# New settings for the virtual clock that orders a fused S4D convolution and channel MLP on one core

## The chip, the core and the metric

The kernel runs on one core of a Trainium2 chip. The metric is the time of one execution on the device in microseconds (us). The core has five engines with a queue each: TensorE (PE in the rows, with its weight loads as PEld), VectorE (DVE), ScalarE (ACT), GpSimd (POOL) and SyncE (SP), which here only starts transfers. An engine works its queue off in order; an instruction that has to wait for another engine or for a transfer holds up all that is queued behind it.

## The reference

For 2048 tokens of 576 channels, `u` is normalized; the normalized rows go through two branches whose product is added to the input:

```python
xn = layernorm(u)                                   # 2048 x 576
A, C = -exp(log_A_real) + 1j*A_imag, (C_real + 1j*C_imag) * dt[:, None]
K = 2 * einsum("dn,dnl->dl", C, exp(A*dt*pos)).real # a filter of 2048 taps for each channel
s = irfft(rfft(xn, 4096) * rfft(K, 4096))[:2048] + xn * D_skip
y = layernorm(xn)
h = gelu(y @ w1 + b1)                               # 576 -> 4608
g = silu(h @ w2 + b2)                               # 4608 -> 576
return u + s * g
```

Everything is float32.

## The kernel before

**The MLP.** The 4608 hidden channels are cut into 12 groups of 384 (`NG`, three blocks of 128 each, `G`), the tokens into two halves of 1024 and each half into two blocks of 512. A *slot* is one group on one block of 512 tokens: there are 48 (`NSLOT`). A slot has eleven *positions*. At the first three, `layer1` (line 633) multiplies a block of `w1` with the tokens, 14 matmuls of 512 columns each. At the other eight, `layer2` (line 707) multiplies the hidden block with `w2`, 72 matmuls of 288 columns in all. Float32 precision is made of two float32r parts, high and low: `w1h`/`w1l`, `XH`/`XL`, `w2h`/`w2l`, `hh`/`hl`. Between the layers ACT makes the GELU (671) and the high part (674), then DVE the low part `hl` (677). DVE adds every finished output to `acc` (717). The weights of each group come in raw and are split by ACT (586) and DVE (583).

**Pairs.** The last 64 of the 576 input channels hold their high part `XR[:64]` and low part `XR[64:]` in one tile. Line 633 therefore ends with two matmuls on `XR`, with `w1r` and with `w1s`. Where `pair` (616) has run before a slot, the first and the third block of this slot leave the `w1s` matmul out: two matmuls of 64 rows each, one on `XR`, one on a copy of its lower half in the tile `bias2`, have done this product already. A pair is made only at the edge of a slot, and only ahead of a visit to the convolution there.

**The convolution.** Between positions TensorE makes *visits*: `kgen` (1042) makes the filter for 16 channels from tables of cosines and magnitudes; `x1` (1157), `k1` (1188), `s2` (1217), `inverse` (1260) and `i1` (1286) transform 96 channels forth and back. Six chunks of 96 channels give 74 visits. A `kgen` may *ride* along in the visit of another kind. The tables are made by DVE (lines 963 to 1003) and ACT (969 to 982); their parameters come by `load_par` (944), started by POOL. The results of a visit go out of PSUM by ACT and by DVE transposes (1165, 1196) or products (1234, 1240). In front of all this stand the layernorms: `BN_STATS` and `BN_AGGR` (423, 425) on DVE, the scaling (466) on POOL.

**What sets the order.** All instructions are written out by the class `Order` before anything runs, and the order is pinned. It keeps a virtual clock for each engine and a price for each step (`dve`, `act`, `pool`, `LEN`); *lines* are chains of steps in order of rank. After each position `advance` lets every step run, in the order in which the clock says it becomes ready, that doesn't delay a more urgent one. `pe_turns` decides whether a visit goes in after a position: its operands must be ready by the clock with a margin, visits of `c1` are paced by `END`, a `kgen` that stands alone waits `ALONE` for company and by `DUE`. `HOLD` puts single steps back by hand. So each of these numbers can move instructions on all engines, and the instructions themselves stay as they are.

Of the kernel before, what the change touches and what calls it, by code (L numbers as in the profile page):

```python
# [32 lines left out]
G = 3  # L33
# [18 lines left out]
class Order:  # L52
# [44 lines left out]
    def take(self, eng, dur, ready, tbl=None):  # L97
        start = max(self.t[eng], ready)
        if eng == "DVE" and self.shared and start < self.t["POOL"] - 0.4:
            dur *= 1.1  # L100
        if tbl and tbl != self.tbl:
            dur += 1.28
            self.tbl = tbl
        self.t[eng] = start + dur
        return start + dur + self.LAT
# [119 lines left out]
def mixer_kernel(ctx, tc, u, log_a_real, a_imag, c_real, c_imag, log_dt, d_skip, w1, b1, w2, b2,  # L225
# [8 lines left out]
    def bank2(name):  # L234
        return ps.tile([P, 2, TB], F32, name=name, bufs=2 if name == "cv" else 1)
# [373 lines left out]
    def pair(tb):  # L609

        Q1[0] = bank2(mx(1))
        for e, x in enumerate((XR[:64, tb], XQ[0][64:])):
            r, k = slice(64 * e, 64 * e + 64), e * (G - 1)
            nc.tensor.matmul(Q1[0][:, e], W[1][3][r, k * P:(k + 1) * P], x, start=True, stop=False,  # L616
                             skip_group_check=True)
        BEGUN.update((0, G - 1))
# [334 lines left out]
    def tables(b):  # L953
# [37 lines left out]
        def weigh(part):  # L991
# [10 lines left out]
            else:  # L1002
# [7 lines left out]
                 step("DVE", dve(SB * NV), f(phase, 0), need=[("kg", b - 2)] if b > 1 else []),  # L1010
                 step("DVE", dve(n), f(phase, 1), hold=HOLD.get(("phase", b), 0)), step("ACT", act(SB * NV), whole),
                 step("DVE", dve(SB * NV), frac, hold=HOLD.get(("frac", b), 0)), step("ACT", act(SB * NV), fold, mark=("fold", b))],
                [step("ACT", act(SB * NV), f(sin, 0), need=[("fold", b)], mark=("sin", b, 0), tbl="sin"),
# [3 lines left out]
                + [step("DVE", dve((2, 2, 1, 1)[part] * n), f(weigh, part), need=[("sin", b, 1)],  # L1017
                        mark=("wu", b) if part == 3 else None, hold=HOLD.get(("weigh", b, part), 0)) for part in range(4)])

# [49 lines left out]
        return behind  # L1069


    X1, S2, INV, I1, KG = 1.5, 1.75, 2.15, 3.05, 1.03

    HOLD = {("weigh", 19, 3): 1, ("phase", 19): 1, ("frac", 18): 2, ("k", 2, 1): (2, 1), (2, 0, 24): 1, (2, 1, 24): 1, ("k1", 2, 1, 2): 1}

    def chunk(c):

# [40 lines left out]
        def in_parts(which, i, get, m, need):  # L1118
# [19 lines left out]
            if which == "x":  # L1138
                four.append(step("ACT", act(2000), turn, need=need))
            hold = HOLD.get((which, c, i), (0, 0))  # L1140
            four.append(step("ACT", act(768), high, need=need if which == "k" else (), hold=hold[0]))
            four.append(step("DVE", dve(768), low, mark=(which + "p", c, i), hold=hold[1]))

        def x1(i):
# [18 lines left out]
            for d0 in (0, 24):  # L1163
                c0 = 48 * i + d0
                add("DVE", 0.9, lambda d0=d0, c0=c0: nc.vector.transpose(
                    A2[:, :, 0, c0:c0 + 24].rearrange("p k d r -> p d k r"), Q[d0]), cv=-1, hold=HOLD.get((c, i, d0), 0))

        def k1(i):
# [26 lines left out]
            for g in (0, 2):  # L1195
                add("DVE", 0.9, lambda g=g: nc.vector.transpose(
                    A2[:, :, 1, 48 * i + 12 * g:48 * i + 12 * g + 24].rearrange("p k d r -> p d k r"), Q[g]), cv=-1,
                    hold=HOLD.get(("k1", c, i, g), 0))

# [118 lines left out]
    NPOS = G + 8  # L1318
    NSLOT = 4 * NG
    od = Order(tc, nc)  # L1320
    od.pinned = True
    el, wl2, wl, nl2, pl, pl2, nl, ml, ml2, xl, wx, c3, c2, c1, c4, kl, tl, sl, vl, gl, odl, fl = [od.line() for _ in range(22)]
    nlh, mlh, mlt = od.line(), od.line(), od.line()
    od.lines = od.lines[-3:] + od.lines[:-3]

# [76 lines left out]


    L1 = 14 * 0.2315
    LEN = [L1] * G + [3 * n * 0.132 + 0.02 for n in (4, 2, 2, 4, 3, 3, 3, 3)]

    T0 = 12.5
    for e, t in dict(PE=0.0, ACT=4.6, DVE=3.7, POOL=3.8, SP=0.0).items():
# [71 lines left out]
    def weigh_in(which):  # L1480

        m = KB + 1 if which == 1 else G
        end = od.t["PE"] + sum(LEN[G:] if which == 1 else LEN[:G])
        for i in range(m):
# [90 lines left out]


    pace = dict(left=NCH * (2 + 2 + 4), last=0.0, started=False)
    END = 1000.0


    EDGE = 0.2, 0.6
    ALONE, DUE = 20.0, (160.0, 950.0)

    def pe_turns(limit=1, any_time=False, all_lines=True, edge=None):
        for x in (nl, pl, ml) + ((c3, c1, kl) if all_lines else ()):
            n = 0
            while n < (2 if x in (c1, nl) else limit):
                h = od.head(x)
                if h is None or h[0]["eng"] != "PE" or h[1] > od.t["PE"] + (0.3 if x is nl else -0.4):
                    break  # L1590
                if x is c1:
                    now = od.t["PE"]
                    gap = (END - now) / max(pace["left"], 1)
                    if n == 0 and pace["started"] and now < pace["last"] + EDGE[edge is None] * gap and not any_time:
                        break
                    pace["started"], pace["last"] = True, now
                    pace["left"] -= 1
                if x is kl and pace["started"]:
                    b = kl["steps"][0]["mark"][1]
                    wait = ("wu", b + 1) not in od.marks or od.t["PE"] < DUE[0] + b * (DUE[1] - DUE[0]) / NB  # L1600
                    if b < NB - 1 and od.t["PE"] < h[1] + (ALONE if wait else 3.0):
                        break
                if edge is not None and not BEGUN and x in (c3, c1, kl):
                    m = wmark(edge // 2, 1) + [("xq", edge)]
                    if all(k in od.marks and od.marks[k] < od.t["PE"] - 0.3 for k in m):
                        od.unit(lambda: pair(edge % 2), 0.24)
                behind = ride(h[0]) if x in (c1, c3) else None
                od.run(x)
                if behind:
                    behind()  # L1610
                od.pin()
                od.advance(od.t["PE"])
                n += 1

    LATER = {}

    def later(slot, pos, f):
        LATER.setdefault((slot, pos), []).append(f)
    mid = 2 * NG
# [19 lines left out]
    def when(pos, q):  # L1639

        return od.t["PE"] + sum(LEN[k % NPOS] for k in range(pos + 1, q))

# [28 lines left out]
    for slot in range(NSLOT):  # L1671
# [3 lines left out]
        n = slot // 2  # L1675
        final = slot >= NSLOT - 2
        for pos in range(NPOS):
            if pos < G:
# [9 lines left out]
                if pos == 2:  # L1688
                    BEGUN.clear()
                    k = slot % (2 * NG)  # L1690
# [16 lines left out]
            else:  # L1707
# [9 lines left out]
                halves = slot == NSLOT - 1 and j == 3  # L1717
                od.unit(lambda: cell.append(layer2(g, tb, j, terms, last, halves or 2 * (slot == NSLOT - 1 and j == 2))), LEN[pos] + 0.95 * (halves and not terms[0][1]), need)
                look_ahead(pos)
                b = 8 + 4 * tb + j  # L1720
                if halves:
                    dh = terms[0][1]
                    od.marks["z", dh] = od.t["PE"] + od.LAT
                    x = od.line()
# [3 lines left out]
                if split:  # L1728
                    add = cell[0]
                    for d in range(2) if j == 0 else (terms[0][1],):  # L1730
# [4 lines left out]
                        x = od.line()  # L1735
# [3 lines left out]
                if last and not halves:  # L1739
# [4 lines left out]
                    elif final:  # L1744
                        x = el if slot < NSLOT - 1 else od.line()
# [10 lines left out]
                if pos == NPOS - 1 and tb == 1 and slot + 1 < NSLOT:  # L1756
                    weigh_in(2)
            for f in LATER.get((slot, pos), ()):
                f()
            od.advance(od.t["PE"])  # L1760
            pe_turns(edge=slot + 1 if pos == NPOS - 1 else None, all_lines=pos in (0, 1, 2, G + 1, G + 3, G + 5, NPOS - 1))
    od.force(lambda: not od.urgent and not any(x["steps"] for x in od.lines))


# [52 lines left out]
```

## Time and profile before

| | |
|---|---|
| median of 3 runs | 1095.59 us (1095.1 to 1095.95) |
| the profiled execution, its own time | 1095.67 us |
| its span, first to last instruction | 1093.9 us |
| PE busy | 1087.1 us (99%) |
| DVE, ACT, POOL busy | 82%, 66%, 17% |
| granted TensorE clock | 0.999 |

The span lies inside the execution's own time, 1.77 us shorter. Matmuls overlap in the profile: the duration of one covers its whole way through the array, and the next starts earlier. What a matmul costs TensorE is the distance from its start to the next start. The timeline shows one instruction or a run of like ones a row, with its start, its duration and, in brackets, what ended an idle stretch before it.

### The profile page before, as it was taken

The page shows a single profiled execution, that of the slowest core. Times are in us where ns is not written, and L with a number is a line of the kernel's source. Part 1 is how long each engine was busy: PE and PEld are TensorE (multiplying, and loading weights), DVE is VectorE, ACT ScalarE, POOL GpSimd, SP SyncE. Part 2 cuts the span into 40 slices and gives each one's busy share as a digit, 9 for nine tenths or more (in the row PEclk, how much of TensorE's full clock was granted, in tenths as well). Part 3 has the DMA queues.
Part 4 walks back from the last instruction along what each step waited for, and adds up shares of the span by engine and source line. Part 5 has one row for each costly group of instructions (what it writes and reads, how often), then busy time and mean ns, then how long its engine had stood idle before and what let it go on. Part 6 is the DMA issues. An engine that isn't in the chain of part 4 may idle for free.

```text
span 1093.9 us, 27052 instructions
## 1 busy us (share of the span) xinstructions
PE 1087.1 (99%) x11445; PEld 954.0 (87%) x11445; DVE 891.9 (82%) x1302; ACT 727.1 (66%) x1113; POOL 188.4 (17%) x261
## 2 busy tenths in 40 slices
PE   9999999999999999999999999999999999999998
PEld 7989899899888898888988888888888888888897
DVE  7798667889998879889899987997969888766367
ACT  6585699778676674767767848685675757534333
POOL 4566210153020100001100000000001021101132
PEclk9999999999999999999999999999999999999999
DMA  8746764626354152355624215143142434454444
GB/s 242 225 149 152 236 235 143 179 80 157 116 160 134 44 112 67 96 110 148 161 48 118 78 56 141 34 122 87 56 126 42 144 101 132 114 170 150 137 151 103
DMA packets 139553, 138.22 MB, mean 126 GB/s; under 512 B 88952, under 2 KB 105016, under 8 KB 138856
## 3 DMA queue, kind: packets, MB, share of 16 engines
q1 hardware_dynamic: 124424, 85.05, 29.0%
q0 software_dynamic: 14528, 50.71, 14.7%
q8 instruction: 89, 1.46, 0.6%
q10 hardware_dynamic: 480, 0.74, 0.3%
q14 instruction: 32, 0.26, 0.1%
HBM read 102.17 MB, written 36.63 MB: 127 GB/s over the span
## 4 chain that ended last, share of the span: by engine, by line
PE 95%; DVE 3%; ACT 1%; SPq 1%; issue 0%; DMA 0%; POOL 0%; DVEq 0%; ACTq 0%; POOLq 0%
PE mxb L707 20%; PE mxa L707 20%; PE mxa L633 20%; PE mxb L633 20%; PE cv L1217 3%; PE cv L1042 3%; PE cv L1260 2%; PE cv L1286 2%; PE cv L1188 1%; PE cv L1157 1%; PE mxa L1348 1%; DVE acc L717 0%; PE mxa L648 0%; SPq L1089 0%; PE mxb L616 0%
## 5 line engine op out<-in xcount | busy, mean ns | idle before, releaser
L677 DVE TENSOR_TENSOR hl<-h,hh 128x512 fp32r<-128x512 f32 x144 | 98.5, 687 | 99.2 <-ACT hh L674 98.4
L707 PE MATMUL mxa<-w2h,hh 128*128 128x288 f32 x573 | 170.3, 297 | 0.0
L707 PE MATMUL mxb<-w2h,hh 128*128 128x288 f32 x573 | 170.2, 297 | 0.0
L707 PE MATMUL mxb<-w2h,hl 128*128 128x288 f32 x573 | 169.3, 295 | 0.1
L707 PE MATMUL mxa<-w2h,hl 128*128 128x288 f32 x573 | 169.1, 295 | 0.0
L707 PE MATMUL mxa<-w2l,hh 128*128 128x288 f32 x573 | 168.6, 294 | 0.0
L707 PE MATMUL mxb<-w2l,hh 128*128 128x288 f32 x573 | 168.6, 294 | 0.0
L671 ACT ACTIVATE h<-mxa,b1t 128x512 f32<-128x512 f32 x73 | 50.1, 687 | 98.3 <-PE mxa L633 95.1
L707 PEld LDWEIGHTS mxa<-w2h,hh 128*128 128x128 f32 x573 | 107.6, 188 | 5.8 <-issue 3.0
L707 PEld LDWEIGHTS mxb<-w2h,hh 128*128 128x128 f32 x573 | 107.6, 188 | 4.3 <-issue 1.4
L707 PEld LDWEIGHTS mxb<-w2l,hh 128*128 128x128 f32 x573 | 107.6, 188 | 0.8
L707 PEld LDWEIGHTS mxa<-w2l,hh 128*128 128x128 f32 x573 | 107.6, 188 | 0.6
L707 PEld LDWEIGHTS mxb<-w2h,hl 128*128 128x128 f32 x573 | 107.5, 188 | 0.3 <-DVE hl L677 0.3
L707 PEld LDWEIGHTS mxa<-w2h,hl 128*128 128x128 f32 x573 | 107.5, 188 | 0.0
L671 ACT ACTIVATE h<-mxb,b1t 128x512 f32<-128x512 f32 x71 | 48.8, 687 | 69.7 <-PE mxb L633 67.2
L674 ACT ACTIVATE hh<-h 128x512 fp32r<-128x512 f32 x144 | 90.7, 631 | 3.7
L944 POOL DMA_DIRECT2D par<-par_s x36 | 27.8, 771 | 367.8 <-DVE mg L988 325.0
L717 DVE TENSOR_TENSOR acc<-mxa,acc 128x576 f32<-128x576 f32 x87 | 65.5, 753 | 26.0 <-PE mxa L707 25.9
L717 DVE TENSOR_TENSOR acc<-mxb,acc 128x576 f32<-128x576 f32 (+1 forms) x89 | 65.9, 741 | 17.8 <-PE mxb L707 17.7
L633 PE MATMUL mxa<-XH,w1h 128*128 128x512 f32 x284 | 79.2, 401 | 0.0
L633 PE MATMUL mxb<-XH,w1h 128*128 128x512 f32 x280 | 77.7, 399 | 0.0
L633 PE MATMUL mxa<-XL,w1h 128*128 128x512 f32 x284 | 76.1, 390 | 0.0
(277 smaller groups left out, 2494.4 us busy)
## 6 DMA issues: line engine op xcount, KB each, us to landing
raw<-in_B_w_dram SPq DMA_DIRECT2D x72, 288.0 KB, 3.4
raw<-in_B_w_dram SPq DMA_DIRECT2D x96, 192.0 KB, 3.5
par_s<-A POOLq DMA_DIRECT2D x4, 2160.0 KB, 8.1
par<-par_s POOLq DMA_DIRECT2D x36, 240.0 KB, 3.6
f2t<-f2q SPq DMA_DIRECT2D x24, 256.0 KB, 3.6
g2t<-g2p SPq DMA_DIRECT2D x24, 256.0 KB, 4.1
bias<-XR SPq DMA_DIRECT2D x42, 128.0 KB, 3.6
raw<-in_B_w_dram SPq DMA_DIRECT2D x48, 96.0 KB, 3.7
```

Source lines behind the costliest of these rows:

```text
L633: nc.tensor.matmul(q, a, b, start=j == 0 and i not in BEGUN, stop=j == len(ops) - 1, skip_group_check=True)
L671: nc.scalar.activation(t, q, AF.Gelu_apprx_tanh, bias=b1t[:, k:k + 1], scale=1.0)
L674: LAST[0] = nc.scalar.activation(hh[:, i], t, AF.Copy)
L677: nc.vector.tensor_sub(hl[:, i], t, hh[:, i].bitcast(F32))
L707: nc.tensor.matmul(q[:, dh, :288], a[:, i, c], b[:, i, d], start=i == 0 and k == 0 and alone != 1, stop=i == G - 1 and k == 2, skip_group_ ...
L717: nc.vector.tensor_add(o, q[:, dh:dh + n, :288], b)
L944: nc.gpsimd.dma_start(PAR[b].rearrange("p (g i) k -> p g (i k)", g=4), dram(par_s, (b // 3 * 48 + b % 3 * 4) * NPAR, [[D * NPAR, P], [12 * ...
L1042: nc.tensor.matmul(q[32 * g:32 * g + 32, i // 2, i % 2 * 64:i % 2 * 64 + 64], U[:, ri, 4 * g + i, :], v[:, ri, 4 * g + i, :], start=ri == ...
L1157: nc.tensor.matmul(Q[24 * v][:, e], FP[0][r, f, 0], x[r, 12 * e:12 * e + 12], start=n == 0, stop=n == 2, skip_group_check=True)
L1217: nc.tensor.matmul(Q[i][32 * q:32 * q + 32, f, ri::2], m[r, 4 * i + q, 32 * ri:32 * ri + 32], A2[r, 4 * p + 2 * i + q // 2, :, :, q % 2], ...
L1260: nc.tensor.matmul(QI[q // 2][64 * f:64 * f + 64, q % 2, i], MAT["g2t", p + i // 2][r, i % 2, f, ri], YS[p + i // 2][0][r, i % 2, ri, f], ...
L1286: nc.tensor.matmul(Q[h][64 * y:64 * y + 64, t], g1t.rearrange("p a e -> p (a e)"), A2[:, k:k + 2, 1].rearrange("p i d r -> p i r d"), star ...
```

## The change

The numbers of the virtual clock are others. DVE beside POOL is priced at 1.05 instead of 1.1; three visit prices change (`X1` 1.55, `S2` 1.68, `INV` 2.34), and that of a pair (0.29); the seven entries of `HOLD` go and one new comes; three pairs of lines change rank (`c1` and `c2`, `kl` and `c4`, `sl` and `tl`); pacing changes (`END`, `ALONE`, `DUE`); a visit's margin is 0.1 instead of 0.4; and visits go in after positions 0, 1, 4, 6 and 10 of a slot, no longer after 2 and 8.

```diff
@@ -97,7 +97,7 @@
         if eng == "DVE" and self.shared and start < self.t["POOL"] - 0.4:
-            dur *= 1.1
+            dur *= 1.05
@@ -1069,9 +1069,9 @@
-    X1, S2, INV, I1, KG = 1.5, 1.75, 2.15, 3.05, 1.03
-
-    HOLD = {("weigh", 19, 3): 1, ("phase", 19): 1, ("frac", 18): 2, ("k", 2, 1): (2, 1), (2, 0, 24): 1, (2, 1, 24): 1, ("k1", 2, 1, 2): 1}
+    X1, S2, INV, I1, KG = 1.55, 1.68, 2.34, 3.05, 1.03
+
+    HOLD = {('k1', 4, 0, 2): 1}
@@ -1319,7 +1319,7 @@
-    el, wl2, wl, nl2, pl, pl2, nl, ml, ml2, xl, wx, c3, c2, c1, c4, kl, tl, sl, vl, gl, odl, fl = [od.line() for _ in range(22)]
+    el, wl2, wl, nl2, pl, pl2, nl, ml, ml2, xl, wx, c3, c1, c2, kl, c4, sl, tl, vl, gl, odl, fl = [od.line() for _ in range(22)]
@@ -1402,7 +1402,7 @@
-    LEN = [L1] * G + [3 * n * 0.132 + 0.02 for n in (4, 2, 2, 4, 3, 3, 3, 3)]
+    LEN = [L1] * G + [3 * n * 0.1319 + 0.02 for n in (4, 2, 2, 4, 3, 3, 3, 3)]
@@ -1575,18 +1575,18 @@
-    END = 1000.0
+    END = 978.0
-    ALONE, DUE = 20.0, (160.0, 950.0)
+    ALONE, DUE = 27.3, (85.0, 852.0)
-                if h is None or h[0]["eng"] != "PE" or h[1] > od.t["PE"] + (0.3 if x is nl else -0.4):
+                if h is None or h[0]["eng"] != "PE" or h[1] > od.t["PE"] + (0.3 if x is nl else -0.1):
@@ -1603,7 +1603,7 @@
-                        od.unit(lambda: pair(edge % 2), 0.24)
+                        od.unit(lambda: pair(edge % 2), 0.29)
@@ -1612,6 +1612,7 @@
+    TURNS = 0, 1, G + 1, G + 3, NPOS - 1,
@@ -1758,7 +1759,7 @@
-            pe_turns(edge=slot + 1 if pos == NPOS - 1 else None, all_lines=pos in (0, 1, 2, G + 1, G + 3, G + 5, NPOS - 1))
+            pe_turns(edge=slot + 1 if pos == NPOS - 1 else None, all_lines=pos in TURNS)
```

No instruction is new. In the built program TensorE has 40 matmuls of line 616 instead of 32, 1934 of line 633 instead of 1942, and the same number of every other line; ACT has 85 table loads instead of 89; the counts of DVE, POOL and SP are equal. TensorE's order is the same up to the start of slot 7 (slots are counted from 0), DVE's up to slot 2.

Three places follow. The first is TensorE at the start of slot 13: the last matmul of slot 12 and what comes next. Before:

```order
L707 MATMUL mxb<-w2h,hl 128x288
L633 MATMUL mxa<-XH,w1h 128x512 x4
L633 MATMUL mxa<-XL,w1h 128x512 x4
L633 MATMUL mxa<-XH,w1l 128x512 x4
L633 MATMUL mxa<-XR,w1r 128x512
L633 MATMUL mxa<-XR,w1s 128x512
L633 MATMUL mxb<-XH,w1h 128x512 x4
L633 MATMUL mxb<-XL,w1h 128x512 x4
L633 MATMUL mxb<-XH,w1l 128x512 x4
L633 MATMUL mxb<-XR,w1r 128x512
L633 MATMUL mxb<-XR,w1s 128x512
L1188 MATMUL cv<-pr,f2t 128x384 x8
```

The same place of TensorE's queue in the changed order:

```order
L707 MATMUL mxb<-w2h,hl 128x288
L616 MATMUL mxa<-XR,w1s 128x512
L616 MATMUL mxa<-bias_773,w1s 128x512
L1042 MATMUL cv<-w 32x64 x32
L1188 MATMUL cv<-pr,f2t 128x384 x8
L1188 MATMUL cv<-ys,f2t 128x384 x8
L1188 MATMUL cv<-pr,f2t 128x384 x8
L633 MATMUL mxa<-XH,w1h 128x512 x4
L633 MATMUL mxa<-XL,w1h 128x512 x4
L633 MATMUL mxa<-XH,w1l 128x512 x4
L633 MATMUL mxa<-XR,w1r 128x512
L633 MATMUL mxb<-XH,w1h 128x512 x4
```

The visit of `k1` has moved from the third position of the slot to its edge, a `kgen` rides with it, and a pair (the two rows of line 616) goes ahead; the first block's `w1s` matmul is gone. Twenty edges have a pair now, sixteen had one.

The second place is DVE in slot 2, where the layernorm statistics of the third quarter of the tokens run beside the MLP (- before, + now; `hl` with 772 is the third hidden block of the slot):

```order
 L425 BN_AGGR mv<-st 128x2
-L423 BN_STATS st<-w 128x6
+L423 BN_STATS st<-w 128x6 x2
+L425 BN_AGGR mv<-st 128x2
 L677 TENSOR_TENSOR hl<-h_772,hh 128x512
-L423 BN_STATS st<-w 128x6
+L423 BN_STATS st<-w 128x6 x2
 L425 BN_AGGR mv<-st 128x2
-L423 BN_STATS st<-w 128x6
```

One `BN_STATS` and one `BN_AGGR` have moved ahead of the third `hl`.

The third place is DVE from the third `hl` of slot 26 on. Before, the rows of `acc` (717) stand ahead of the next table (963):

```order
L677 TENSOR_TENSOR hl_6931<-h32_7068,hh_6930 128x512
L972 TENSOR_TENSOR w_7047<-w_7047 128x16x65
L988 TENSOR_TENSOR mg_7185<-par_6886 128x16x64
L988 TENSOR_TENSOR mg_7185<-par_6886 128x16x32
L717 TENSOR_TENSOR acc_82<-mxa_7082,acc_82 128x576
L717 TENSOR_TENSOR acc_82<-mxb_7097,acc_82 128x576
L1234 TENSOR_TENSOR pr_7217<-cv_7107,kk_7202 128x768
L1240 TENSOR_TENSOR ys_7228<-pr_7217 128x2x2x96
L963 TENSOR_TENSOR w_7230<-par_7176,tv_76 128x16x65
```

In the changed order, from the same `hl` on:

```order
L677 TENSOR_TENSOR hl_7108<-h32_7169,hh_7107 128x512
L1001 TENSOR_TENSOR w_6936<-w_6936,mg_7083 128x16x32
L1003 SCALAR_TENSOR_TENSOR w_6936<-w_6936,mg_7083 128x16x32
L988 TENSOR_TENSOR mg_7272<-par_7011 128x16x64
L988 TENSOR_TENSOR mg_7272<-par_7011 128x16x32
L963 TENSOR_TENSOR w_7359<-par_7270,tv_76 128x16x65
L717 TENSOR_TENSOR acc_82<-mxa_7255,acc_82 128x576
L1234 TENSOR_TENSOR pr_7378<-cv_7284,kk_7362 128x768
L717 TENSOR_TENSOR acc_82<-mxb_7275,acc_82 128x576
```

The table's row 963, which reads the parameters that a transfer of POOL brings, now stands ahead of both `acc` rows of this slot. On POOL, the transfer is queued in both orders behind a small copy (679) that waits for this same `hl`.

## Rows read from the trace of the kernel before

**Rows 1.** The page, part 1: busy us, share of the span and instructions of each engine.

```profile
PE 1087.1 (99%) x11445; PEld 954.0 (87%) x11445; DVE 891.9 (82%) x1302; ACT 727.1 (66%) x1113; POOL 188.4 (17%) x261
```

**Rows 2.** Waits of PE in the whole span, the longer one: total, times, longest.

```profile
PE mxa L1348 <- POOL XL L1341: 1.3, 1, 1.3
```

**Rows 3.** Timeline of PE, end of layer 1 in slot 26: start us, duration, instruction.

```profile
588.63 0.39 PE L633 MATMUL mxb<-XR,w1r 128*128 128x512 f32 x1
588.86 0.39 PE L633 MATMUL mxb<-XR,w1s 128*128 128x512 f32 x1
```

**Rows 4.** Timeline of PE around a visit of k1 with a pair, and without one.

```profile
958.15 0.29 PE L707 MATMUL mxa<-w2h,hl 128*128 128x288 f32 x1
...
960.08 0.50 PE L633 MATMUL mxb<-XH,w1h 128*128 128x512 f32 x1
...
949.54 0.29 PE L707 MATMUL mxa<-w2h,hl 128*128 128x288 f32 x1
...
951.04 0.40 PE L707 MATMUL mxb<-w2h,hh 128*128 128x288 f32 x1
```

**Rows 5.** Timeline of PE around a visit of x1 with a pair, and without one.

```profile
672.25 0.29 PE L707 MATMUL mxa<-w2h,hl 128*128 128x288 f32 x1
...
673.96 0.50 PE L633 MATMUL mxb<-XH,w1h 128*128 128x512 f32 x1
...
549.33 0.29 PE L707 MATMUL mxa<-w2h,hl 128*128 128x288 f32 x1
...
550.80 0.40 PE L707 MATMUL mxb<-w2h,hh 128*128 128x288 f32 x1
```

**Rows 6.** Timeline of DVE and PE in slot 2, around its third hl.

```profile
62.41 0.21 DVE L425 BATCH_NORM_AGGREGATE mv<-st 128x2 f32<-128x12 f32 x1
62.53 0.64 DVE L677 TENSOR_TENSOR hl<-h,hh 128x512 fp32r<-128x512 f32 x1
...
64.18 0.46 DVE L423 BATCH_NORM_STATS2 st<-w 128x6 f32<-128x288 f32 x1
64.55 0.68 DVE L677 TENSOR_TENSOR hl<-h,hh 128x512 fp32r<-128x512 f32 x1
...
65.37 0.29 PE L707 MATMUL mxa<-w2l,hh 128*128 128x288 f32 x1
65.50 0.29 PE L707 MATMUL mxa<-w2h,hl 128*128 128x288 f32 x1
```

**Rows 7.** Timeline of DVE and PE in slot 25, around its third hl.

```profile
566.35 1.23 DVE L963 TENSOR_TENSOR w<-par,tv 128x1040 f32<-128x1040 f32 x1
567.50 0.69 DVE L677 TENSOR_TENSOR hl<-h,hh 128x512 fp32r<-128x512 f32 x1
...
567.86 0.29 PE L707 MATMUL mxb<-w2l,hh 128*128 128x288 f32 x1
568.24 0.40 PE L707 MATMUL mxb<-w2h,hl 128*128 128x288 f32 x1
```

**Rows 8.** POOL behind slot 26's third hl; line 944's landings from 500 us; the page's acc group.

```profile
592.22 1.13 POOL L679 COPY tv<-hl 128x1 f32<-128x1 f32 x1 [30.63 <-DVE hl L677]
593.30 0.75 POOL L944 DMA_DIRECT2D par<-par_s  x1
...
DMA to landing us min/median/max: 3.2/3.5/6.0
...
L717 DVE TENSOR_TENSOR acc<-mxa,acc 128x576 f32<-128x576 f32 x87 | 65.5, 753 | 26.0 <-PE mxa L707 25.9
```

**Rows 9.** Timeline of PE: a visit of kgen with s2, and one of the inverse.

```profile
591.32 0.29 PE L707 MATMUL mxb<-w2h,hl 128*128 128x288 f32 x1
...
594.12 0.40 PE L707 MATMUL mxa<-w2h,hh 128*128 128x288 f32 x1
...
604.34 0.39 PE L633 MATMUL mxa<-XR,w1s 128*128 128x512 f32 x1
...
606.42 0.97 PE L633 MATMUL mxb<-XH,w1h 128*128 128x512 f32 x3
```

## Prediction, made before the changed kernel ran

> **What bounds the kernel now.** I read the page's busy times first, then TensorE's waits, then its timeline. TensorE is busy for 1087.1 of 1093.9 us [rows 1], and the longer of its two recorded waits, 1.3 us, lies before the first matmul of the warm-up [rows 2]. No other engine is near: DVE stands at 82%. But a busy TensorE may hide short waits, since each matmul is drawn over its whole way through the array, so I went through the distances from one start to the next. A matmul of 512 columns costs 0.23 us [rows 3], one of 288 columns 0.13 us [rows 6], and nearly every distance in the MLP is of this size. What is above it stands next to a visit to the convolution, or is one short wait in slot 25. So the time is the sum of TensorE's own work. An order can win by having TensorE do less, by cheaper switches between MLP and convolution, and by the few tenths that are left of waits; and it can lose wherever it puts something ahead of a step for which TensorE has only just enough time.
>
> **What the change does to TensorE's own work.** Before and after there are 74 visits, eight of them of a `kgen` alone, so the number of switches is the same. Of the rides, one goes from a visit of `k1` to one of `i1`; a `kgen` costs the same beside either, so far as the trace tells, and I put that at nothing. What differs is the pairs: 20 instead of 16. One pair takes out two matmuls of line 633, 2 x 0.23 = 0.46 us. What it puts in is read from visits with and without one. With `k1`: 960.08 - 958.15 = 1.93 us from the last matmul before to the first behind, against 951.04 - 949.54 = 1.50 us; the pair costs 0.43 us [rows 4]. With `x1`: 673.96 - 672.25 = 1.71 against 550.80 - 549.33 = 1.47; it costs 0.24 us [rows 5]. So a pair is worth 0.46 - 0.24 = 0.22 us ahead of `x1` and 0.46 - 0.43 = 0.03 us ahead of `k1`; for the other kinds I take the price of `k1`. By the built order, 5 of the 16 stood ahead of an `x1`, and 6 of the 20 do. The gain is 0.22 + 3 x 0.03 = 0.31 us. Its bounds are four pairs at 0.03 and at 0.22: 0.1 to 0.9 us.
>
> The Trainium skill has a rule on this, in TensorEngine Tiling (Array Packing), Theoretical Speedup: with a contraction of up to 64 rows, two tiles share the array and the work may go up to twice as fast. By that alone a pair would cost one matmul, any host would do, and four more pairs would save 0.91 us, for a time of 1094.9. The same page, Key Properties, says that a change of the tiling mode drains the engine; the rows agree with this one, since a pair is cheap where `x1` follows, whose matmuls are 64 rows high too, and dear ahead of `k1`, whose matmuls have 32 rows.
>
> **Slot 2, the statistics ahead of `hl`.** In the order before, the third `hl` starts at 64.55 and ends at 65.23; the matmul that needs it starts at 65.50, in step with its neighbour at 65.37 [rows 6]. In slot 25 an `hl` ended at 567.50 + 0.69 = 568.19 and the matmul that had waited for it started at 568.24 [rows 7]: 0.05 us is what the signal takes. The margin in slot 2 is thus 65.50 - 65.23 - 0.05 = 0.22 us. Now a `BN_STATS` goes ahead, 64.55 - 64.18 = 0.37 us from start to start, and a `BN_AGGR`, 0.12 us up to an `hl` behind it (62.41 to 62.53); since the aggregation reads what the statistics write, it can't overlap with them, and 0.1 us more goes there (0.46 - 0.37) [rows 6]. `hl` comes 0.59 us later. TensorE waits 0.59 - 0.22 = 0.37 us. Nothing hides that: the queue behind is TensorE's own. Bounds 0.15 (if the aggregation overlaps and the margin is a little larger) to 0.6.
>
> **Slot 25, a wait that goes.** Before, the start of a table, line 963 with 1.23 us, stood directly ahead of the third `hl`, and TensorE started at 568.24 what it would have started at 567.86 + 0.13 = 567.99 [rows 7]. In the changed order of this slot no line 963 stands there, only two shorter steps (1001, 1003), and the visits around it are others. I take the whole 0.25 us as won; bounds 0 and 0.25.
>
> **The rest of the order.** Some 1800 lines of DVE's order differ. Where they move a step that TensorE doesn't wait for, nothing follows. A further gain can't be large, for the waits that it would have to come from aren't there [rows 2]; a further loss is bounded by the size of slot 2's, about 0.37 us a place. ACT loses four table loads; it isn't waited for. SP's transfers of weights move with the splits that free their buffers, and TensorE shows no wait for weights before. The last visit stands a quarter of a slot earlier than before, with almost four slots of MLP behind it in both, so the end of the program, where TensorE is the last to hand over, is untouched.
>
> **The sum.** -0.31 (pairs) + 0.37 (slot 2) - 0.25 (slot 25) = -0.19 us. The profiled execution took 1095.67 us, 0.08 above the median of the three runs, so 1095.67 - 0.19 = 1095.48: **1095.5 us**. With the bounds of the three terms, -0.9 to +0.5, this is 1094.8 to 1096.2. About 0.2%, 2.2 us, is what a measurement of this kernel can tell from no change; the forecast is no change.
>
> **Rival 1, parameters that come late (slower).** In slot 26 a copy on POOL waits for the third `hl`, and the transfer of the next parameters is queued behind it: 593.30 - 592.22 + 0.05 = 1.13 us from the end of `hl` to its start, and 3.2 to 6.0 us to its landing, 3.5 in the median [rows 8]. Before, the table that reads them (963) stands behind both `acc` rows; now it stands ahead of them, and a late landing holds up `acc`, which frees the PSUM bank for TensorE. Counted from the start of the last matmul of layer 1: `hl` ended 592.17 - 588.86 = 3.3 us later before [rows 3, 8], some of it behind work that the new order puts elsewhere; I estimate 2.5 to 3.3. Then 1.13, the landing, 1.23 for the table [rows 7], 0.75 for `acc` [rows 8] and a little: ready after 5.6 to 6.4 us plus the landing. TensorE needs the bank after an inverse (2.08 from 604.34), 35 matmuls of 0.13 and a `kgen` with `s2` (2.80 from 591.32) [rows 6, 9]: 2.08 + 4.55 + 2.80 + 0.2 = 9.6 us. It decides at a landing of 3.2 to 4.0 us. At 3.5 the wait is between nothing and 0.3 us, at 6.0 between 2.0 and 2.8: 1097.5 to 1098.3. For it: one place, and a median close to the point. Against it: the landing must be among the longest.
>
> **Rival 2, slot 2 in many places (slower).** Seven steps that were held back by hand run free now, and visits may go in 0.3 us earlier by the clock. If that lets seven steps in ahead of an `hl` or a GELU as in slot 2, it is 7 x 0.37 = 2.6 us: 1098.1. It decides from a delay of 0.22 us in each. Against it: steps ahead of `hl` are allowed by the clock only where it sees room, and its prices are close to the rows.
>
> **Rival 3, all pairs at full worth (faster).** If the host's kind made no difference, all four new pairs would save 0.22 us; with no loss in slot 2 (its margin would have to be 0.6 us instead of 0.22) and the wait of slot 25 gone, the change is 4 x (-0.22) - 0.25 = -1.13 us: 1094.5. Against it are the two visits with `k1` [rows 4].
>
> **How the numbers follow.** Forecast 0.80, rival 1 0.08 (half of it past the bound of 0.2%), rival 2 0.07 (most of it past), rival 3 0.05 (within the bound). Faster by over 0.2% would need 2.2 us out of waits that aren't there; I leave 0.02 for what I don't see. Slower by over 0.2%: 0.04 + 0.05 = 0.09. Within: 0.89. The range takes in the bounds of the terms, rival 3 down to 1094.5, and rival 1 up to some 1.7 us of wait: 1094.5 to 1097.2.
>
> **What would show it.** In the changed profile 20 + 20 matmuls of line 616, with 0.24 us ahead of `x1` and 0.43 elsewhere; in slot 2 a matmul that starts about 0.4 us behind its step, right after `hl`; no such step in slot 25; in slot 26 line 963 directly behind the landing and TensorE in step behind it. A row of GELUs or `hl` that TensorE waits for would make rival 2 right. A pair ahead of `s2` or `inverse` that costs 0.24 would make rival 3 right.

## The result: 0.2% slower, by one wait of TensorE

The changed kernel takes 1097.26 us in the median of 16 runs (1096.73 to 1100.31), the kernel before 1095.34 us in 16 runs beside it (1094.75 to 1095.95). The ratio is 1.0021, with an interval of 1.0014 to 1.0028: 1.9 us slower. That is 0.06 us above the upper end of the predicted range, and 1.8 us above the predicted time. The spread is also another: from lowest to highest 3.6 us, before 1.2.

The profiled execution of the changed kernel took 1097.61 us, its span is 1095.8 us (before 1095.67 and 1093.9). The busy times of the page, part 1, in the order of [rows 1], hardly differ from before:

```profile
PE 1086.8 (99%) x11445; PEld 953.1 (87%) x11445; DVE 889.9 (81%) x1302; ACT 722.5 (66%) x1109; POOL 188.1 (17%) x261
```

TensorE's waits tell more. They answer to [rows 2]; the columns are the total, the number of waits and the longest:

```profile
PE mxb L633 <- ACT h L671: 1.5, 1, 1.5
...
PE mxa L707 <- DVE hl L677: 0.2, 1, 0.2
```

The first row is new and is the longest of the program: a matmul of layer 1 waited for a GELU on ACT. The last row is the wait in slot 2 that the prediction has. The three left out belong to the start.

The chain of waits around the first row shows what the GELU was late for (start us, duration, piece):

```profile
247.64 0.42 SPq L1089
...
248.85 2.06 SPq L1089
...
250.95 5.66 DMA xc<-xn_s
...
256.79 2.12 ACT xt L1124
...
258.92 1.28 ACT L671
...
260.22 0.69 ACT h L671
...
260.96 1.20 PE mxb L633 x4
```

SPq is SP's queue, and ACT's row of line 671 without a tile is the load of the GELU's table. SP's queue issues the four transfers of the convolution's next input (`load`, line 1089) over 4.8 us; the last of them starts 3.3 us after the first and takes 5.66 us to land. ACT's step `turn` (1124) waits for it, needs 2.12 us, then ACT loads the GELU's table, 1.28, and only then runs slot 12's first GELU. TensorE's third block of the slot goes into the same tile `mxb` as the first, and it waited until this GELU had read the first. TensorE had started the last matmul of the second block at 259.08 and could have gone on at 259.08 + 0.23 = 259.31; it went on at 260.96, 1.65 us later. Its timeline (start us, duration, instruction, and in brackets what ended the idle time before it):

```profile
259.08 0.39 PE L633 MATMUL mxa<-XR,w1s 128*128 128x512 f32 x1
260.96 0.50 PE L633 MATMUL mxb<-XH,w1h 128*128 128x512 f32 x1 [1.49 <-ACT h L671]
```

In the kernel before, the same step 1124 stands behind the GELUs of this slot. From the timeline of ACT before:

```profile
256.41 0.69 ACT L671 ACTIVATE h<-mxb,b1t 128x512 f32<-128x512 f32 x1
...
262.59 2.10 ACT L1124 ACTIVATE xt<-xc 128x768 f32<-128x768 f32 x1
```

In the changed kernel it stands ahead of them, and ACT idles for 2.16 us until its data are there. From the timeline of ACT after:

```profile
253.55 1.08 ACT L969 ACTIVATE w<-w 128x1040 int32<-128x1040 f32 x1
256.79 2.12 ACT L1124 ACTIVATE xt<-xc 128x768 f32<-128x768 f32 x1 [2.16 <-DMA xc<-xn_s]
```

**Where the 1.9 us are.** The start of the program differs from execution to execution, so I compare a stretch, D: from the start of the first matmul of line 633 (34.04 us before, 34.86 after) to the start of the last of line 707. D holds nearly all that an order can do to TensorE. In it I count the matmuls of the MLP at 0.2266 us (512 columns) and 0.1324 (288), and for each of the 74 visits what it adds to the distance between the matmuls around it, up to the third matmul behind it. A second trace of each kernel (two of the experiments below) gives D again:

| | D, us | what it consists of |
|---|---|---|
| before | 1054.52, 1054.07 | matmuls and visits 1052.33 and 1052.05; slot 25's wait 0.24 in both |
| after | 1055.72, 1055.82 | matmuls and visits 1051.89 and 1051.91; slot 2's wait 0.34 in both; slot 12's wait 1.65 and 1.75 |

What is left is 1.8 to 2.0 us in all four. Most of it, 1.4 to 1.6 us, is that away from waits and visits a matmul of 512 columns takes 0.2275 us in the mean and not the 0.2266 that it is counted at. The means differ by 1055.77 - 1054.30 = 1.47 us: -0.29 from the matmuls and visits (the pairs), -0.24 from slot 25, +0.34 from slot 2, +1.70 from slot 12, and a rest of -0.04. The first of these is hardly larger than the 0.28 us between the two traces of before; the waits are the same in both traces of a kernel to 0.1 us. The medians differ by 1.9 us and, beside the second trace, by 1.6; what they have beyond the 1.47 is not accounted for.

### The profile page after: what moved, and what is told of

It reads as the page before. It is cut to its first block, busy times and chain, and to the rows that moved or that the text cites. A ratio compares the mean times of both kernels' runs of the same rounds, so it can differ in the third digit from the quotient of the medians.

```text
span 1095.8 us, 27057 instructions
## 1 busy us (share of the span) xinstructions
PE 1086.8 (99%) x11445; PEld 953.1 (87%) x11445; DVE 889.9 (81%) x1302; ACT 722.5 (66%) x1109; POOL 188.1 (17%) x261
## 4 chain that ended last, share of the span: by engine, by line
PE 95%; DVE 2%; DMA 1%; ACT 1%; SPq 0%; issue 0%; ACTq 0%; DVEq 0%
PE mxb L707 20%; PE mxa L707 20%; PE mxa L633 20%; PE mxb L633 20%; PE cv L1042 3%; PE cv L1217 3%; PE cv L1260 2%; PE cv L1286 2%; PE cv L1188 1%; PE cv L1157 1%; DMA xc<-xn_s 1%; DMA acc<-in_A_u_dram 1%; PE mxa L616 0%; PE mxa L648 0%; PE mxb L616 0%; PE cv L516 0%
```

## The experiments

Theory A is: the loss is slot 12's wait, and this comes from one step of ACT that the new order puts ahead of a GELU together with a transfer that lands late. The rivals are that the wait belongs to one execution, that the step alone or the transfer alone does it, and that the loss is spread over the program. In the recorded expectations that follow, the letters stand for the theories of that one experiment.

**1. The changed kernel, with the step behind the GELU.** Two entries of `HOLD` put the step back by two places on ACT:

```diff
-    HOLD = {('k1', 4, 0, 2): 1}
+    HOLD = {('k1', 4, 0, 2): 1, ('turn', 0, 1): 2, ('x', 0, 1): (1, 0)}
@@
-                four.append(step("ACT", act(2000), turn, need=need))
+                four.append(step("ACT", act(2000), turn, need=need, hold=HOLD.get(("turn", c, i), 0)))
```

> The changed kernel with one step moved on ACT: the scaling of the transform's input (line 1124) that stood ahead of slot 12's first GELU now stands behind this GELU and its high part; all other queues are as in the changed kernel. Theory A (the GELU, and with it TensorE, waited 1.65 us for this step, which had itself waited for a late transfer): the gap of TensorE at 259 us closes, and the time falls by 1.5 to 1.7 us, to about 1095.6, with a spread from run to run as small as that of the kernel before. Theory B (that wait belongs to the profiled execution alone, and the loss of 1.9 us is spread over the program or lies in its start): the time stays at 1097.0 to 1097.3.

Measured: 1095.19 us (1094.94 to 1095.60) beside 1094.97 for the kernel before, ratio 1.0002 (0.9993 to 1.0010). The GELU now comes as soon as TensorE has handed over, and TensorE goes on without a gap. The timeline of this experiment, ACT and then TensorE:

```profile
255.35 0.69 ACT L671 ACTIVATE h<-mxb,b1t 128x512 f32<-128x512 f32 x1 [0.41 <-PE mxb L633]
...
256.61 2.09 ACT L1124 ACTIVATE xt<-xc 128x768 f32<-128x768 f32 x1
...
258.10 0.39 PE L633 MATMUL mxa<-XR,w1s 128*128 128x512 f32 x1
258.33 0.84 PE L633 MATMUL mxb<-XH,w1h 128*128 128x512 f32 x3
```

The transfers are as late here as in the changed kernel, so a late transfer alone costs nothing. Their times from issue to landing:

```profile
DMA to landing us min/median/max: 5.0/5.9/7.3
```

D is 1054.08 us, 1.7 less than with the wait. As far as the times can tell (to about 1 us), the whole loss hung on the place of one step on ACT. The long tail of the times goes with it: the highest of 11 runs is 0.4 us above the median, where the changed kernel has 3.0. A single high run is no sign of this wait, though: the kernel before has one in experiment 5, 2.2 us above its median.

**2. The changed kernel, with less traffic beside the transfer.** Eleven copies that POOL starts from 245 to 251.5 us go behind its next transfer of parameters; nothing else moves.

```diff
-        gl["steps"].append(step("POOL", 2.8, lambda j=j: order_mats(j)))
+        gl["steps"].append(step("POOL", 2.8, lambda j=j: HQ["q"].append(lambda: order_mats(j)) if HQ["on"] else order_mats(j)))
...
-        gl["steps"].append(step("POOL", 0.7, lambda b=b: order_u(b)))
+        gl["steps"].append(step("POOL", 0.7, lambda b=b: HQ["q"].append(lambda: order_u(b)) if HQ["on"] else order_u(b)))
```

(`HQ["on"]` is set by `load_par(7)`; `load_par(8)` empties the list.)

> The changed kernel with its order on DVE, ACT, SP and TensorE kept; on POOL eleven copies from DRAM to DRAM (eight of line 333, three of line 358), which ran from 245 to 251.5 us beside the transfer of the transform's input, are issued behind the next transfer of parameters, at about 272 us. Theory A1 (the transfer landed late because these copies shared the DMA engines with it): it lands 1 to 2 us earlier, at 254.6 to 255.6 us, TensorE's gap shrinks from 1.65 to at most 0.5 us, time 1095.6 to 1096.2. Theory A2 (the transfer is slow by itself: four transfers in short rows, issued one behind the other over 4.8 us): it lands as late as before, at 256 to 257 us, and the time stays at 1096.9 to 1097.3.

Measured: 1095.35 us (1094.93 to 1095.88), ratio 1.0002 (0.9993 to 1.0012). ACT's order is that of the changed kernel, with the step ahead of the GELU, and yet the gap is gone. The timeline, ACT and then TensorE:

```profile
252.56 1.08 ACT L969 ACTIVATE w<-w 128x1040 int32<-128x1040 f32 x1
253.54 2.10 ACT L1124 ACTIVATE xt<-xc 128x768 f32<-128x768 f32 x1
...
258.09 0.39 PE L633 MATMUL mxa<-XR,w1s 128*128 128x512 f32 x1
258.32 0.84 PE L633 MATMUL mxb<-XH,w1h 128*128 128x512 f32 x3
```

The step follows 969 with no idle time, so its data were there by 253.5 us. The times from issue to landing of the four transfers of line 1089, in the changed kernel:

```profile
DMA to landing us min/median/max: 5.4/5.6/6.7
```

The same in this experiment:

```profile
DMA to landing us min/median/max: 3.6/4.5/4.8
```

SP issues them faster too: the first to the last in 2.7 us instead of 3.3. From the first issue to the last landing it is 6.3 us here, and 8.6 to 9.1 in the five traces with the copies beside it (the changed kernel's two, and those of experiments 1, 4 and 7). This is what theory A1 says, and more than it expected: 2.7 us sooner and not 1 to 2, and a time below its 1095.6 to 1096.2. So in the changed kernel the wait needs both halves: with the transfer in time, the step ahead of the GELU costs nothing.

**3. The kernel before, with the step ahead of the GELU.** The step is called directly behind line 982, and nothing else moves.

```diff
-                nc.scalar.activation(w, w, AF.Sin, scale=TWO_PI)
+                nc.scalar.activation(w, w, AF.Sin, scale=TWO_PI); b == 5 and PULL.pop()()
@@
-                four.append(step("ACT", act(2000), turn, need=need))
+                four.append(step("ACT", act(2000), (PULL.append(turn) or (lambda: None)) if (c, i) == (0, 1) else turn, need=need))
```

> The kernel before with one step moved on ACT alone: the same scaling (line 1124) goes from behind slot 12's GELUs to ahead of the first of them, as in the changed kernel. Theory A: the step takes 2.1 us, the table load behind it 1.28; from 255.1 us (end of line 982) the GELU ends at 259.2, and TensorE, which needs it at 258.2, waits 1.0 to 1.2 us even if the transfer is in time: time 1096.4 to 1096.6. Theory B (one such step can't set the time): 1095.3, as the kernel before.

Measured: 1095.99 us (1095.44 to 1097.02) beside 1094.97, ratio 1.0011 (1.0002 to 1.0020). The timeline, ACT and then TensorE:

```profile
255.28 2.09 ACT L1124 ACTIVATE xt<-xc 128x768 f32<-128x768 f32 x1
...
258.69 0.69 ACT L671 ACTIVATE h<-mxb,b1t 128x512 f32<-128x512 f32 x1
...
258.25 0.39 PE L633 MATMUL mxa<-XR,w1s 128*128 128x512 f32 x1
259.43 0.50 PE L633 MATMUL mxb<-XH,w1h 128*128 128x512 f32 x1 [0.79 <-ACT h L671]
```

Here the data are in time: the step has no idle time before it. But it starts only 3.2 us ahead of TensorE's need (255.28 to 258.25 + 0.23 = 258.48), where experiment 2 had 4.8 (253.54 to 258.32), and it takes 4.1 us from there to the GELU's end. So it costs 259.43 - 258.48 = 0.95 us. The sum of the expectation (end of 982, step, table load and GELU against TensorE's need) gave 1.0 to 1.2. The time lies below the expected 1096.4 to 1096.6, which was counted from 1095.3 for the kernel before; beside 1094.97 it is 1.02 us more. So the step alone can cost time too, where it starts late enough.

**4. Both places mended.** The first experiment's kernel, and in slot 2 the statistics behind `hl`:

```diff
-                                        hold=int((b0, t, i) in ((8, 1, 0), (8, 2, 1), (8, 3, 0)))))
+                                        hold=int((b0, t, i) in ((8, 1, 0), (8, 2, 1), (8, 3, 0), (12, 2, 1)))))
```

> The first experiment's kernel (scaling behind the GELU), and in slot 2 one BN_STATS and the BN_AGGR back behind the third hl, as in the kernel before. Theory A: beyond the first experiment 0.35 to 0.45 us is gained in slot 2 (the gap of 0.34 us at 66.2 us and the tenth that the matmul behind it takes longer), so about 1095.2, within 0.3 us of the kernel before; the pairs, 0.3 to 0.4 us, and slot 25, 0.35, would even put it at 1094.7 if the start costs the same. Theory B (statistics ahead of hl don't matter, since the wait would come back at the next hl): no difference to the first experiment.

Measured: 1094.97 us (1094.30 to 1095.39) beside 1094.97, ratio 0.9998 (0.9989 to 1.0007). Slot 2's gap is closed. TensorE's timeline around it in the first experiment, with the gap:

```profile
65.21 0.29 PE L707 MATMUL mxa<-w2l,hh 128*128 128x288 f32 x1
65.69 0.40 PE L707 MATMUL mxa<-w2h,hl 128*128 128x288 f32 x1 [0.20 <-DVE hl L677]
```

The same two matmuls in this experiment:

```profile
65.35 0.29 PE L707 MATMUL mxa<-w2l,hh 128*128 128x288 f32 x1
65.48 0.29 PE L707 MATMUL mxa<-w2h,hl 128*128 128x288 f32 x1
```

D is 1053.68 us, 0.40 less than in the first experiment and 0.4 to 0.8 less than in the traces of the kernel before. Within D no wait above 0.15 us is left between matmuls of the MLP. The times cannot tell 0.4 us from nothing, so this is no version that is shown to beat the kernel before.

**5. The kernel before, a second trace.**

> The kernel before, unchanged, for a second trace. From TensorE's first matmul of layer 2 to its last the first trace has 1066.15 us. Theory A (the order's own time, waits of TensorE aside, is the same in each execution, and only the start and the landing of transfers vary): 1066.0 to 1066.3 again, with the wait of 0.24 us in slot 25; the first matmul of layer 2 may start anywhere from 21.9 to 22.9 us. Theory B (the first trace was a slow one of this kernel, by some tenths within the steady part): 1065.3 to 1065.8.

Measured: 1095.05 us (1094.56 to 1097.29) beside 1095.07. From first to last matmul of layer 2 it is 1065.70 us, 0.45 less than in the first trace. Slot 25's wait is there again, 0.24 us, so theory A holds for the waits; but the matmuls and visits differ by 0.28 us between two executions of one order, and D by 0.45, and in this theory B was right. A difference of a few tenths in D between two single traces is therefore not evidence.

**6. The changed kernel, a second trace.**

> The changed kernel, unchanged, for a second trace and more times. Theory A (the gap ahead of slot 12's second block is as long as the transfer of the transform's input is late): a gap again at the same matmul, of 1.0 to 4 us, from first to last matmul of layer 2 1066.06 us and the gap (1067.71 and 1.65 in the first trace), and ACT's step 1124 directly behind the landing; median 1096.7 to 1097.5. Theory B (the gap was of that one execution): no gap, median 1095.2.

Measured: 1096.71 us (1096.42 to 1099.64) beside 1095.07, ratio 1.0018 (1.0009 to 1.0027). The gap is there again, 1.75 us (from 258.04 to 260.01, less the 0.2266 of one matmul), and the step again stands directly behind the landing. The timelines of ACT and of TensorE, and the transfers' times to landing:

```profile
255.85 2.11 ACT L1124 ACTIVATE xt<-xc 128x768 f32<-128x768 f32 x1 [2.27 <-DMA xc<-xn_s]
...
258.04 0.39 PE L633 MATMUL mxa<-XR,w1s 128*128 128x512 f32 x1
260.01 1.20 PE L633 MATMUL mxb<-XH,w1h 128*128 128x512 f32 x4 [1.59 <-ACT h L671]
...
DMA to landing us min/median/max: 4.3/5.9/7.4
```

From first to last matmul of layer 2 it is 1067.45 us, 0.36 less than the expected 1066.06 and the gap; a difference of this size is what experiment 5 has between two traces of one order.

**7. Pairs only ahead of x1.** The fourth experiment's kernel; `pair` leaves its two matmuls out unless the host is an `x1`, and the clock counts as before, so that all else keeps its place.

```diff
-                        od.unit(lambda: pair(edge % 2), 0.29)
+                        od.unit(lambda: pair(edge % 2, h[0]["mark"][0] == "x1"), 0.29)
```

> The kernel of the fourth experiment (both places mended) with pairs only at the six edges where x1 is the host; at the other fourteen the two matmuls of line 616 are left out and those of line 633 put back, 28 more there and 28 fewer of 616; the clock, and so the order of all else, is unchanged. Theory A (rows of the trace: a pair costs 0.43 us ahead of k1, s2, inverse, i1 and kgen, and takes out 0.45): 14 x 0.03 = 0.4 us slower, from first to last matmul of layer 2 1065.7 us against 1065.31, time 1095.2 to 1095.5. Theory B (two tiles that share the array cost one matmul wherever they stand): 14 x 0.23 = 3.2 us slower, 1068.5 us from first to last, time about 1098.2.

Measured: 1095.28 us (1094.74 to 1096.85), ratio 1.0003 (0.9994 to 1.0012). D is 1054.03 against 1053.68 us, 0.35 us for fourteen pairs, 0.025 us each. This agrees with theory A but doesn't measure it, since two traces of one order differ by as much. Theory B's 3.2 us are out. (From the first matmul of layer 2 it is 1066.02, above the expected 1065.7, because slot 0 took 0.37 us more; D leaves slot 0 out.)

**8. The changed kernel, with one setting undone.** It asks whether one of the settings is to blame, and whether the others are harmless:

```diff
-            dur *= 1.05
+            dur *= 1.1
```

> The changed kernel with one of its settings undone: DVE beside POOL is priced at 1.1 again instead of 1.05; all other settings stay. The built order has the step of line 1124 behind all three GELUs of slot 12, and 16 pairs. Theory A (the loss of the changed kernel is that one place, and the other settings cost nothing that can be measured): no gap at slot 12, from the first matmul of slot 1 to the last of layer 2 1053.9 to 1054.6 us (1054.52 and 1054.07 in the two traces of the kernel before, 1055.72 and 1055.83 in those of the changed one), time 1094.9 to 1095.4. Theory B (the lower margin and the other settings let steps in ahead of GELUs and of hl wherever the order happens to put them): one or more other gaps of 0.3 to 1.7 us in its place, time 1095.6 to 1097.5.

Measured: 1100.64 us (1100.00 to 1101.06) beside 1095.33, ratio 1.0048 (1.0032 to 1.0065): 5.3 us slower than the kernel before, where the changed kernel is 1.6 to 1.9 us slower. The step of line 1124 is behind the GELUs and slot 12 has no gap, as theory A has it, and no gap between matmuls of the MLP has taken its place, against theory B; but the time is far above what either had. The loss has another form: ten visits of a lone `kgen` instead of eight, two visits that take 0.9 and 0.4 us longer than their like, and an end that is 3.1 us longer. D is 1056.17 us, 1.9 more than in the mean of the kernel before; with the end, this is 5.0 of the 5.3 us. The last visit, an `i1`, has its last matmuls at 1027.6 us, 14 us later than in the changed kernel; POOL then still loads and stores rows of the convolution when the last outputs go out. The end of POOL's timeline in the changed kernel:

```profile
1089.42 1.04 POOL L826 DMA_DIRECT2D out_dram<-w  x2 [0.57 <-DVE w L820]
```

The same in this experiment:

```profile
1089.71 2.08 POOL L758 DMA_DIRECT2D out_dram<-row  x4 [0.95 <-DVE row L755]
1091.78 1.04 POOL L826 DMA_DIRECT2D out_dram<-w  x2
```

From the end of the last matmul to the end of the span it is 8.1 us instead of 4.9. The last to land in both is a store of line 826: it is issued at 1093.8 instead of 1092.6, and it and its neighbours take longer. The times from issue to landing of this line's last stores, in the changed kernel and then here:

```profile
DMA to landing us min/median/max: 2.2/2.3/2.6
...
DMA to landing us min/median/max: 2.4/4.0/4.5
```

That POOL's late rows are what slows them is likely, but no run shows it. The seven entries of `HOLD` that the change drops did not by themselves let the step in: they are gone here too, and the step stands behind the GELUs. The settings hang together: undoing this one moves the step to where it costs nothing, and 5.3 us are lost elsewhere.

## Why the prediction was wrong

**The pairs: right in the rows, and too small to show in the times.** The forecast was -0.31 us with 0.03 for a pair ahead of other hosts than `x1`. The matmuls and visits changed by -0.29 us in the mean of two traces each, and experiment 7 has 0.025 a pair, but both are differences that two traces of one order can have. What carries the price are the visits themselves, which take the same time to a few hundredths of a us wherever they recur. Visits of the changed kernel that answer to [rows 4], an inverse with a pair and one without, in TensorE's timeline:

```profile
322.49 0.29 PE L707 MATMUL mxb<-w2h,hl 128*128 128x288 f32 x1
...
324.90 0.50 PE L633 MATMUL mxa<-XH,w1h 128*128 128x512 f32 x1
...
455.65 0.29 PE L707 MATMUL mxb<-w2h,hl 128*128 128x288 f32 x1
...
457.63 0.40 PE L707 MATMUL mxa<-w2h,hh 128*128 128x288 f32 x1
```

2.41 - 1.98 = 0.43 us ahead of the inverse; ahead of `x1` it is 0.24 again, as in [rows 5] (917.96 to 919.67 against 531.55 to 533.02). The price of `k1`, taken for the kinds that had no row, was right, and rival 3 is out. The rule of the Trainium skill that a pair may go up to twice as fast (TensorEngine Tiling (Array Packing), Theoretical Speedup) comes nearly true ahead of `x1`, where a pair costs 0.24 us and one full matmul 0.23, and not ahead of the others. The prediction laid this to the height of the host's matmuls, 64 rows against 32. That is not the whole of it: the matmuls of `s2` are 64 rows high too, and a pair costs about 0.44 us ahead of them. In the changed kernel's trace a visit of `s2` adds 2.17 - 0.13 = 2.04 us with a pair (963.48 to 965.65, behind a matmul of 288 columns) and 1.83 - 0.23 = 1.60 without (976.65 to 978.48, behind one of 512). In the timeline the pair and `x1` have the shape 64*128, `s2` has 64*32; only the host with the pair's own shape gets it cheap.

**Slot 2: right.** A wait of 0.37 us was forecast; it is 0.34, and 0.1 for the next matmul. The rows of the changed kernel that answer to [rows 6], DVE and then TensorE:

```profile
65.01 0.82 DVE L423 BATCH_NORM_STATS2 st<-w 128x6 f32<-128x288 f32 x2
...
65.99 0.64 DVE L677 TENSOR_TENSOR hl<-h,hh 128x512 fp32r<-128x512 f32 x1
...
66.21 0.29 PE L707 MATMUL mxa<-w2l,hh 128*128 128x288 f32 x1
66.68 0.40 PE L707 MATMUL mxa<-w2h,hl 128*128 128x288 f32 x1 [0.18 <-DVE hl L677]
66.92 0.30 PE L707 MATMUL mxa<-w2h,hh 128*128 128x288 f32 x1
```

**Slot 25: right.** The wait of 0.25 us of [rows 7] is gone; from slot 13 to the end the changed kernel has no wait between matmuls of the MLP.

**The sum: right for what it held.** -0.19 us was forecast. Without slot 12's wait, in experiment 1, D is 1054.08 us against 1054.30 in the mean of the two traces of before: -0.22. The two differ by 0.45, so this agrees with the forecast and doesn't confirm it. One figure in the working is off: the three lower bounds add up to -0.9 + 0.15 - 0.25 = -1.0 and not to -0.9. The stated range is not touched by it.

**Rival 1: the mechanism, at another place.** It said that a transfer which lands late would hold up a step standing ahead of one that TensorE needs, put it at slot 26 and gave it 0.08. In slot 26 the parameters landed as the median has it, and the table followed at once. The timeline of the changed kernel, POOL and then DVE:

```profile
596.89 0.75 POOL L944 DMA_DIRECT2D par<-par_s  x1
...
600.57 1.24 DVE L963 TENSOR_TENSOR w<-par,tv 128x1040 f32<-128x1040 f32 x1 [1.20 <-DMA par<-par_s]
602.16 0.76 DVE L717 TENSOR_TENSOR acc<-mxa,acc 128x576 f32<-128x576 f32 x1 [0.34 <-PE mxa L707]
```

`acc` waited for TensorE there, not for the table. What the rival described happened on ACT, in slot 12, with another transfer. The top of the stated range, 1097.2, was set by some 1.7 us of this rival's wait; that the measured median lies only 0.06 us above it is luck, for the wait of 1.65 to 1.75 us is another one.

**Rival 2: right in kind, wrong in number.** It said that steps let in ahead of an `hl` or a GELU make TensorE wait, in seven places at 0.37 us, and gave this 0.07. Its sign, a GELU that TensorE waits for, is there. But besides slot 2 there is one such place and not seven, and it costs four to five times as much.

**The step that failed** is "The rest of the order": "a further loss is bounded by the size of slot 2's, about 0.37 us a place", and of ACT, "it isn't waited for". Both were read from the waits of before, where indeed no GELU is waited for. But these waits say what the old order let happen. The changed order had to be asked anew, engine by engine, and the order of ACT I had not laid beside that of before as I did for DVE. There the step of line 1124 stood ahead of slot 12's first GELU, and its price could be had from rows of before: 2.10 for the step, 1.28 for the table load, 0.69 for the GELU, 4.1 us with what lies between. For TensorE's need at 259.3 us the step had to start by 255.1, 4 us behind the last issue at 251.0. The transfer took 5.66. The other half was lateness, and it was missing too: the landing of this transfer I had not read, though the trace of before has it:

```profile
DMA to landing us min/median/max: 4.0/4.9/5.8
```

So the bound of a place is not the size of one known wait, but the length of the longest step that stands ahead of a needed one, with the table load that it pushes back and the lateness of its data. With 5.8 us for the landing this place comes to 251.0 + 5.8 + 4.1 - 259.3 = 1.6 us; the issue at 251.0 and the need at 259.3 are those of the changed kernel's trace, and ahead of it they would have had to be estimated. The runs show 1.65 and 1.75 us at this one place, more than four times the bound, and experiment 1 that the loss goes when the wait goes.

**Why the clock put it there.** The step that loads the data is written as `step(None, 5.0, lambda: load(i + 1))`: four transfers, taken as landed 5.0 us after the step. SP's queue started the last of them 3.3 us after the first, and this one needed 5.66 more, 9.0 us in all (247.64 to 256.61). The planner advances no clock for SP's queue and has none for the traffic of POOL's copies, so it counts 5.0 us where 9.0 went by. This is read from the code: no run changes the price, so that a truer one would have kept the step behind the GELU is not shown.

## What to carry to other kernels

When an order changes, list for every engine each step that has newly come ahead of one that the bounding engine needs, and price it as step + the table load still to come behind it + lateness of its data; a wait list of the old order is no bound for the new one. A step that reads a transfer is the dangerous kind: put it behind the urgent step, where its lateness costs nothing, as two entries of `HOLD` do here. A planner that treats a transfer as a fixed delay should at least add the time until its queue reaches the last of them, here 3.3 us for four transfers.

## What was not expected of the hardware

The start of the program, where the order on TensorE and DVE is the same in all these kernels, takes a different time in each execution: over ten traces the first matmul of slot 1 starts from 33.80 to 34.86 us. The 0.82 us by which the changed kernel's first trace started later than that of the kernel before is such a difference; its second trace started at 33.80.

Copies between places in DRAM that POOL starts slow the transfers that SP issues, even though the queues are different: the four transfers of 96 KB land after 4.3 to 7.4 us in the five traces with eleven copies beside them, in the median of each trace 5.6 to 5.9, and after 3.6 to 4.8 us, in the median 4.5, in the one trace without. The Trainium skill (DMA: Bandwidth & Descriptors, Issuing engines are not separate DMA queues) states that transfers from all issuing engines end up on the same 16 DMA engines and interleave; experiment 2 agrees. I had not drawn on it.

A matmul behind a wait takes a tenth of a us longer, on top of the wait itself: 66.92 - 66.68 = 0.24 us instead of 0.13. The first matmul behind a visit does so too: 0.34 us for one of 512 columns in place of 0.23, and over the 74 visits this comes to some 8 us of TensorE's time.
